# Attention's sink products: two passes over 128 rows in place of three over 64

## The chip, the cores and the metric

The kernel runs on one core of a Trainium2 chip. The metric is the device time of one execution in microseconds (us), as the median of several runs. The engines are named as in the profile: PE is TensorE (matmuls), PEld its weight loads, DVE is VectorE, ACT is ScalarE, POOL is GpSimd, SP issues most DMAs. Each engine runs its own instructions in the order in which the program gives them, and waits on semaphores for the others.

## The reference

Three stages follow each other: attention with a window and sinks, a mixture of experts weighted by a Sinkhorn iteration, and a top-1 mixture of experts. Only the first is touched:

```python
# q, k, v: (2, 8, 768, 64); n_sink = 4, window = 128
scores = scale * np.matmul(q, k.transpose(0, 1, 3, 2))
keep = is_sink | in_window          # pos < n_sink, or 0 <= row - col < window
scores = np.where(keep, scores, -1e9)
a = np.exp(scores - np.max(scores, axis=-1, keepdims=True))
a = a / (np.sum(a, axis=-1, keepdims=True) + 1e-09)
attn_out = np.matmul(a, v)
```

The two mixtures then work on `attn_out` as 1536 tokens of 512 numbers, with 8 experts of 512x1024 and 1024x512 each.

## The kernel before

**High and low parts.** A product of two fp32 operands is made of three matmuls in fp32r. Each operand is kept as a high part (a copy rounded to fp32r, made by ACT or DVE) and a low part (operand minus high part, made by DVE or POOL). `mm3` (lines 65 to 68) then adds low x high (line 66), high x low (67) and high x high (68) into one PSUM tile. Every product in attention and in the mixtures goes through it, so lines 66 to 68 stand for all matmuls of this kind, and one tells them apart by the tiles.

**Attention** runs over 12 blocks of 128 queries (6 in each of the 2 batches), and in each block over 4 pairs of heads. One pair is one step `m`, 48 in all. From the third block of a batch on, a query sees 128 + 128 window keys and SK = 16 sink keys, so the scores are 272 wide (256 or 128 wide before). A step is spread over several turns of the loop (lines 1201 to 1245): in the turn of `m`, PE does

1. `pv(m - 5)`, the products of the probabilities with the values, into the one PSUM tile `pv`. It takes four heads of a group, two in each of two turns (part 0 and part 1). After part 1, ACT copies it to `xh` (line 1172) and DVE makes `xl` from it; the next part 0 can't start ahead of that, since it writes the same tile;
2. `p_trans(m - 3)`, four transposes of P into `tr`, after which ACT makes the high part and DVE the low part (tiles called `pt` or `acc` in the profile);
3. in odd turns `s_trans(m - 2)` (line 1138), the transpose of the sink columns `pk` of four heads at once into the PSUM tile L1; in even turns the transposes of the next block's k or q (line 1003), through the same PSUM tile L1. ACT makes `skh`, `kh` or `qh` from it, DVE makes `skl`, `kl` or `ql`; only after that is L1 free for the next transpose;
4. `scores(m)`, six matmuls for two heads (`sc`), from which DVE takes the row minimum (line 1096) and ACT the exponential (line 1100).

The subtractions for the low parts are not emitted where they arise but gathered (`defer`) and emitted by `flush()` (line 992) after `pv` and `norm`, and again after `scores`. `norm(m - 1)` has DVE make the reciprocal of the row sums (lines 1108, 1109), POOL multiply P by it (line 1111) and POOL copy the 16 sink columns of the two heads into `pk` (line 73, called by `pcopy`).

**The sink products.** For each head of a block with sinks, `pv` adds the 16 sink keys' share as one more `mm3` (line 1164): the stationary operand is `vsh` or `vsl`, 64 rows (4 heads x 16 sinks, of which only the own head's 16 rows hold values, the others zero) by 64 columns; the moving operand is `skh` or `skl`, 64 rows by 128 queries. There are 2 batches x 4 blocks x 8 heads = 64 heads of this kind. `vsh` and `vsl` are made once a batch by `prep_vs`.

**Fills.** In turns from `m` = 21 on, the first mixture's matmuls (tiles `L` and `y`, 512 columns) stand between attention's, one group of three in five of six places of two turns (line 1295). Ahead of that, and in a turn where a unit has ended, PE has attention alone. What is left of these units, and all that follows, comes after attention.

Of the kernel before, what the change touches and what calls it, by code (L numbers as in the profile page):

```python
# [8 lines left out]
F32 = mybir.dt.float32  # L9
F32R = mybir.dt.float32r  # L10
I32 = mybir.dt.int32
AF = mybir.ActivationFunctionType
ALU = mybir.AluOpType
# [10 lines left out]
def kernel(  # L24
# [15 lines left out]
    nc = tc.nc  # L40
    B, H, S, D = q.shape
# [9 lines left out]
    SK = 16  # L51
# [11 lines left out]
    ps_m = ctx.enter_context(tc.tile_pool(name="ps_m", bufs=1, space=PSUM))  # L63

    def mm3(out_ap, ah, al, bh, bl, start, stop):
        nc.tensor.matmul(out_ap, al, bh, start=start, stop=False)  # L66
        nc.tensor.matmul(out_ap, ah, bl, start=False, stop=False)  # L67
        nc.tensor.matmul(out_ap, ah, bh, start=False, stop=stop)  # L68

    def pcopy(dst, src):  # L70
        a = src if src.dtype == F32 else src.bitcast(F32)
        o = one[0:a.shape[0], :].unsqueeze(2).to_broadcast(list(a.shape))
        nc.gpsimd.tensor_tensor(dst, a, o, op=ALU.mult)

    def ctile(shape, name, dt=F32):
        return const.tile(shape, dt, name=name)
# [3 lines left out]

    ident = ctile([128, 128], "ident")
    one = ctile([128, 1], "one")
    rflag = ctile([128, 1], "rflag")
    iof = ctile([128, 128], "iof")
    x2d = dram.tile([N, DM], F32, name="x2d")
# [718 lines left out]
    a1 = att.enter_context(tc.tile_pool(name="a1", bufs=1))  # L804
    a2 = att.enter_context(tc.tile_pool(name="a2", bufs=2))
# [183 lines left out]
    def defer(*args):  # L989
        later.append(args)  # L990
# [6 lines left out]
    kt, qt, vt, vs = [], {}, {}, {}  # L997
# [52 lines left out]
        return r  # L1050

    def prep_vs(b, r):
        sh = a1.tile([4 * SK, 2, 4, D], F32R, name="vsh")
        sl = a1.tile([4 * SK, 2, 4, D], F32R, name="vsl")
        full = accp.tile([4 * SK, 2, 4, D], F32, name="acc7")
        for g in range(2):
            nc.gpsimd.tensor_tensor(
                full[:, g], r[:, g, :].unsqueeze(1).to_broadcast([4 * SK, 4, D]),
                bdiag.unsqueeze(2).to_broadcast([4 * SK, 4, D]), op=ALU.mult,
            )  # L1060
        vs[b] = sh, sl

        def fin():
            nc.vector.tensor_copy(sh, full)
            nc.vector.tensor_tensor(sl, full, sh.bitcast(F32), op=ALU.subtract)
            acc[7] = accp.tile([128, DM], F32, name="acc7")

        return fin

    P, sums, pts = {}, {}, {}  # L1070

    def width(i):
        return (128, 256, 256 + SK)[min(i, 2)]

    def where(m):
        blk, pr = divmod(m, 4)
        b, i = divmod(blk, NB)
        return blk, b, i, pr
# [25 lines left out]
    def norm(m):  # L1104
        blk, b, i, pr = where(m)
        w = width(i)
        rs = a3.tile([128, 2], F32, name="rs")
        nc.vector.tensor_scalar(rs, sums.pop(m), 1e-9, None, op0=ALU.add)
        nc.vector.reciprocal(rs, rs)
        p = P[m][:, :, 0:w]  # L1110
        nc.gpsimd.tensor_tensor(p, p, rs.unsqueeze(2).to_broadcast([128, 2, w]), op=ALU.mult)
        if i >= 2:
            if pr % 2 == 0:
                pts[m // 2, "k"] = a2.tile([128, 4, SK], F32, name="pk")
            o = 2 * (pr % 2)
            pcopy(pts[m // 2, "k"][:, o:o + 2, :], P[m][:, :, 128:128 + SK])

    def p_trans(m):
        blk, b, i, pr = where(m)
# [12 lines left out]
    def s_trans(m):  # L1132
        blk, b, i, pr = where(m)
        if i < 2:
            return
        pk = pts.pop((m // 2, "k"))
        ph = ps_m.tile([4 * SK, 128], F32, name="L1", tag="L1")
        nc.tensor.transpose(ph, pk.rearrange("p h s -> p (h s)"), ident)
        th = a2.tile([4 * SK, 128], F32R, name="skh")
        tl = a2.tile([4 * SK, 128], F32R, name="skl")  # L1140
        nc.scalar.activation(th, ph, AF.Copy)
        defer(tl, ph, th)
        pts[m // 2, "s"] = th, tl

    def pv(m):
        blk, b, i, pr = where(m)
        g, part = divmod(pr, 2)
        o = pvt
        sink = i >= 2
        nch = 1 if i == 0 else 2  # L1150
        th, tl = pts.pop(m)
        for hh in range(2):
            j = 2 * part + hh
            hs = slice((4 * g + j) * D, (4 * g + j + 1) * D)
            for c in range(nch):
                vh, vl = vt[blk if c == nch - 1 else blk - 1]
                mm3(
                    o[:, j, :], vh[:, hs], vl[:, hs], th[:, hh, c, :], tl[:, hh, c, :],
                    c == 0, c == nch - 1 and not sink,
                )  # L1160
            if sink:
                sth, stl = pts[m // 2, "s"]
                sh, sl = vs[b]
                mm3(o[:, j, :], sh[:, g, j, :], sl[:, g, j, :], sth, stl, False, True)
        if part == 0:
            return
        c, t = divmod(blk, TPC)
        cs = slice(t * 128, (t + 1) * 128)
        for r in range(2):
            ps = slice(64 * r, 64 * r + 64)  # L1170
            oh = xh[c][ps, 2 * g:2 * g + 2, cs]
            nc.scalar.activation(oh, o[:, r::2, :], AF.Copy)
            defer(xl[c][ps, 2 * g:2 * g + 2, cs], o[:, r::2, :], oh)
# [4 lines left out]
    def attention():  # L1178
# [22 lines left out]
        for m in range(NM + LV):  # L1201
            blk, pr = divmod(m, 4)
            if m >= LV:
                pv(m - LV)
            if 1 <= m <= NM:
                norm(m - 1)
# [4 lines left out]
            if 2 < m <= NM + 1 and m % 2 == 1:  # L1211
                s_trans(m - 2)
# [19 lines left out]
            if m % (4 * NB) == 8:  # L1232
                vfin = prep_vs(blk // NB, vsr.pop(blk // NB))
# [216 lines left out]
```

## Time and profile before

| | us |
|---|---|
| median of 3 runs | 1479.87 (1479.65 to 1479.95) |
| profiled execution, its own time | 1480.35 |
| its span, first to last instruction | 1478.6 |
| PE busy | 1442.5 (98% of the span) |
| DVE busy | 695.2 (47%) |
| ACT busy | 455.5 (31%) |
| POOL busy | 129.8 (9%) |

Attention takes the first 206 us of the span; in it the sink products stand from 51.9 us (batch 0, to 109.7 us) and from 141.6 us (batch 1, to 204.4 us). The fills begin at 79.0 us. The busy time of PE counts each matmul from its start to the end of its way through the array. Matmuls overlap, so the cost of one in a row of them is the distance from its start to the next one's start, and that is read from the timeline, not from the duration.

In the profile a matmul's form such as `128*64 128x128` means: 128 rows and 64 columns of the array in use, and 128 partitions by 128 columns streamed through it.

### The profile page before, as it was taken

The page shows a single profiled execution, that of the slowest core. Times are in us where ns is not written, and L with a number is a line of the kernel's source. Part 1 is how long each engine was busy: PE and PEld are TensorE (multiplying, and loading weights), DVE is VectorE, ACT ScalarE, POOL GpSimd, SP SyncE. Part 2 cuts the span into 40 slices and gives each one's busy share as a digit, 9 for nine tenths or more (in the row PEclk, how much of TensorE's full clock was granted, in tenths as well). Part 3 has the DMA queues.
Part 4 walks back from the last instruction along what each step waited for, and adds up shares of the span by engine and source line. Part 5 has one row for each costly group of instructions (what it writes and reads, how often), then busy time and mean ns, then how long its engine had stood idle before and what let it go on. Part 6 is the DMA issues. An engine that isn't in the chain of part 4 may idle for free. (4 is left out here: it accounts for less than half of the span.)

```text
span 1478.6 us, 18476 instructions
## 1 busy us (share of the span) xinstructions
PE 1442.5 (98%) x7245; PEld 1178.2 (80%) x7245; DVE 695.2 (47%) x1487; ACT 455.5 (31%) x966; POOL 129.8 (9%) x188
## 2 busy tenths in 40 slices
PE   5899999999999999999999999999999999899998
PEld 4777787788888888888888888888888877788886
DVE  5868643553323333332423333242333257877774
ACT  4756532111202211120211112021111133666664
POOL 3634310000000000000000000000000000111111
PEclk9999999999999999999999999999999999999999
DMA  5412102000101010010101000010100041987771
GB/s 110 95 44 59 44 30 86 29 29 29 57 0 58 0 57 29 29 51 7 58 1 57 28 30 31 27 57 1 57 0 0 29 143 44 327 278 263 269 259 56
DMA packets 86029, 105.69 MB, mean 71 GB/s; under 512 B 41518, under 2 KB 41518, under 8 KB 85936
## 3 DMA queue, kind: packets, MB, share of 16 engines
q1 hardware_dynamic: 83056, 96.58, 20.4%
q0 software_dynamic: 2880, 7.87, 1.6%
q8 instruction: 59, 0.97, 0.3%
q14 instruction: 34, 0.28, 0.1%
HBM read 101.29 MB, written 7.86 MB: 74 GB/s over the span
## 5 line engine op out<-in xcount | busy, mean ns | idle before, releaser
L192 ACT ACTIVATE hh<-L 128x512 fp32r<-128x512 f32 x192 | 114.8, 598 | 802.0 <-PE L L68 801.9
L193 DVE SCALAR_TENSOR_TENSOR hl<-L,hh 128x512 fp32r<-128x512 f32 x192 | 132.8, 692 | 355.9 <-ACT hh L192 355.7
L216 DVE SCALAR_TENSOR_TENSOR acc<-y,Pm,acc 128x512 f32<-128x512 f32 x168 | 126.1, 751 | 252.3 <-PE y L68 251.9
L66 PE MATMUL y<-whb,hl 128*128 128x512 f32 x432 | 170.8, 395 | 0.0
L68 PE MATMUL y<-whb,hh 128*128 128x512 f32 x432 | 168.6, 390 | 0.0
L67 PE MATMUL y<-wlb,hh 128*128 128x512 f32 x432 | 168.2, 389 | 0.0
L66 PE MATMUL y<-wha,hl 128*128 128x512 f32 x412 | 163.0, 396 | 0.1
L68 PE MATMUL y<-wha,hh 128*128 128x512 f32 x412 | 160.6, 390 | 0.0
L67 PE MATMUL y<-wla,hh 128*128 128x512 f32 x412 | 160.5, 390 | 0.0
L66 PE MATMUL L<-xh,wla 128*128 128x512 f32 x384 | 152.8, 398 | 0.0
L66 PE MATMUL L<-xh,wlb 128*128 128x512 f32 x384 | 151.0, 393 | 0.0
L68 PE MATMUL L<-xh,wha 128*128 128x512 f32 x384 | 149.7, 390 | 0.0
L68 PE MATMUL L<-xh,whb 128*128 128x512 f32 x384 | 149.6, 390 | 0.0
L67 PE MATMUL L<-xl,wha 128*128 128x512 f32 x384 | 149.6, 390 | 0.0
L67 PE MATMUL L<-xl,whb 128*128 128x512 f32 x384 | 149.6, 390 | 0.0
L68 PEld LDWEIGHTS y<-whb,hh 128*128 128x128 f32 x432 | 81.1, 188 | 17.2
L67 PEld LDWEIGHTS y<-wlb,hh 128*128 128x128 f32 x432 | 81.2, 188 | 16.0
L66 PEld LDWEIGHTS y<-whb,hl 128*128 128x128 f32 x432 | 81.2, 188 | 16.0
L688 POOL DMA_INDIRECT acc<-x2d,ig_s x2 | 2.1, 1051 | 1045.7 <-DVE tmp_d L439 1020.5
L68 PEld LDWEIGHTS y<-wha,hh 128*128 128x128 f32 x412 | 77.4, 188 | 16.1
L66 PEld LDWEIGHTS y<-wha,hl 128*128 128x128 f32 x412 | 77.4, 188 | 15.8 <-DVE acc L210 0.2
L67 PEld LDWEIGHTS y<-wla,hh 128*128 128x128 f32 x412 | 77.5, 188 | 15.0
(313 smaller groups left out, 2358.2 us busy)
## 6 DMA issues: line engine op xcount, KB each, us to landing
raw<-in_moe_w SPq DMA_DIRECT2D x80, 1024.0 KB, 5.5
raw<-in_v SPq DMA_DIRECT2D x12, 256.0 KB, 2.9
raw<-vfb SPq DMA_DIRECT2D x12, 256.0 KB
x2d<-acc SPq DMA_DIRECT2D x12, 256.0 KB, 2.0
raw<-in_k SPq DMA_DIRECT2D x11, 256.0 KB
raw<-in_q SPq DMA_DIRECT2D x11, 256.0 KB, 6.1
raw<-in_k SPq DMA_DIRECT2D x2, 128.0 KB
raw<-in_q SPq DMA_DIRECT2D x2, 128.0 KB
```

What stands on the lines that cost most here:

```text
L66: nc.tensor.matmul(out_ap, al, bh, start=start, stop=False)
L67: nc.tensor.matmul(out_ap, ah, bl, start=False, stop=False)
L68: nc.tensor.matmul(out_ap, ah, bh, start=False, stop=stop)
L192: nc.scalar.activation(hh, ps, AF.Relu)
L193: nc.vector.scalar_tensor_tensor(hl, ps, 0.0, hh.bitcast(F32), op0=ALU.max, op1=ALU.subtract)
L216: nc.vector.scalar_tensor_tensor(a, ps, Pm[:, blk, e:e + 1], a, op0=ALU.mult, op1=ALU.add)
L688: nc.gpsimd.indirect_dma_start(out=x, out_offset=None, in_=src, in_offset=bass.IndirectOffsetOnAxis(ap=index(ig_s, ig_d, i), axis=0))
```

## The change

The values of the sinks are kept in one tile `vsk` of 128 rows: rows 0 to 63 hold the high parts, rows 64 to 127 the low parts. POOL writes the sink probabilities twice into `pk` (now 2 x 4 x 16 = 128 columns), so that the transpose gives 128 rows, in which rows 64 to 127 repeat rows 0 to 63; `skh` and `skl` have 128 rows each. A product of all 128 rows with `skl`, and one with `skh`, added up, gives (high + low) x low + (high + low) x high. So each head has two matmuls of 128 rows by 64 columns, first with `skl`, then with `skh`, where there were three of 64 by 64. The product low x low, left out before, is in it.

```diff
     def prep_vs(b, r):
-        sh = a1.tile([4 * SK, 2, 4, D], F32R, name="vsh")
-        sl = a1.tile([4 * SK, 2, 4, D], F32R, name="vsl")
+
+        t = a1.tile([128, 2, 4, D], F32R, name="vsk")
...
-            nc.vector.tensor_copy(sh, full)
-            nc.vector.tensor_tensor(sl, full, sh.bitcast(F32), op=ALU.subtract)
+            hi = t[0:4 * SK]
+            nc.vector.tensor_copy(hi, full)
+            nc.vector.tensor_tensor(t[4 * SK:128], full, hi.bitcast(F32), op=ALU.subtract)
...
-                pts[m // 2, "k"] = a2.tile([128, 4, SK], F32, name="pk")
+                pts[m // 2, "k"] = a2.tile([128, 2, 4, SK], F32, name="pk")
             o = 2 * (pr % 2)
-            pcopy(pts[m // 2, "k"][:, o:o + 2, :], P[m][:, :, 128:128 + SK])
+            pk = pts[m // 2, "k"][:, :, o:o + 2, :]
+            src = P[m][:, :, 128:128 + SK].unsqueeze(1).to_broadcast([128, 2, 2, SK])
+            nc.gpsimd.tensor_tensor(pk, src, one3.to_broadcast([128, 2, 2, SK]), op=ALU.mult)
...
-        ph = ps_m.tile([4 * SK, 128], F32, name="L1", tag="L1")
-        nc.tensor.transpose(ph, pk.rearrange("p h s -> p (h s)"), ident)
-        th = a2.tile([4 * SK, 128], F32R, name="skh")
-        tl = a2.tile([4 * SK, 128], F32R, name="skl")
+        ph = ps_m.tile([128, 128], F32, name="L1", tag="L1")
+        nc.tensor.transpose(ph, pk.rearrange("p c h s -> p (c h s)"), ident)
+        th = a2.tile([128, 128], F32R, name="skh")
+        tl = a2.tile([128, 128], F32R, name="skl")
...
-                sth, stl = pts[m // 2, "s"]
-                sh, sl = vs[b]
-                mm3(o[:, j, :], sh[:, g, j, :], sl[:, g, j, :], sth, stl, False, True)
+                for n, a in enumerate(pts[m // 2, "s"][::-1]):
+                    nc.tensor.matmul(o[:, j, :], vs[b][:, g, j, :], a, start=False, stop=n == 1)
```

No instruction changes its place but for the sink matmuls themselves. On PE, in the third head with sinks and the start of the fourth, in the order of the program (engine PE, `pv` of one turn; `pt_1211` and `acc_1212` are the high and low part of the transposed probabilities), before:

```order
L66 MATMUL pv<-pt_1211,vl 64x128
L67 MATMUL pv<-acc_1212,vh 64x128
L68 MATMUL pv<-pt_1211,vh 64x128
L66 MATMUL pv<-skh,vsl 64x128
L67 MATMUL pv<-skl,vsh 64x128
L68 MATMUL pv<-skh,vsh 64x128
L66 MATMUL pv<-pt_1211,vl 64x128
L67 MATMUL pv<-acc_1212,vh 64x128
```

And now, at the same place (`pt_1208` and `acc_1209` are the same two tiles):

```order
L66 MATMUL pv<-pt_1208,vl 64x128
L67 MATMUL pv<-acc_1209,vh 64x128
L68 MATMUL pv<-pt_1208,vh 64x128
L1167 MATMUL pv<-skl,vsk 64x128
L1167 MATMUL pv<-skh,vsk 64x128
L66 MATMUL pv<-pt_1208,vl 64x128
L67 MATMUL pv<-acc_1209,vh 64x128
```

One of three sink matmuls is gone, and the first of the two left reads `skl`, which DVE writes, where the first of the three read `skh`, which ACT writes.

## Rows read from the trace of the kernel before

**Rows 1.** The page's first part: busy us, share of the span, instructions of each engine.

```profile
PE 1442.5 (98%) x7245; PEld 1178.2 (80%) x7245; DVE 695.2 (47%) x1487; ACT 455.5 (31%) x966; POOL 129.8 (9%) x188
```

**Rows 2.** PE's timeline, first sink head: start, duration, tiles, rows*columns, idle before.

```profile
51.78 0.23 PE L68 MATMUL pv<-acc,vh 128*64 128x128 f32 x1
51.94 0.27 PE L66 MATMUL pv<-skh,vsl 64*64 64x128 f32 x1
52.05 0.22 PE L67 MATMUL pv<-skl,vsh 64*64 64x128 f32 x1
...
52.25 0.28 PE L66 MATMUL pv<-acc,vl 128*64 128x128 f32 x1
52.37 0.22 PE L67 MATMUL pv<-acc,vh 128*64 128x128 f32 x1
52.43 0.22 PE L68 MATMUL pv<-acc,vh 128*64 128x128 f32 x1
```

**Rows 3.** Stretches: busy us and (instructions) of tile skh alone, clock, DMA.

```profile
51.40:77.40 26.00, 6.23 (x32) 3.97 (x32) 1.09 (x4) 1.03 (x4) 1.00 0.29 64
```

**Rows 4.** PE's timeline in two turns without fills.

```profile
57.91 0.24 PE L66 MATMUL pv<-pt,vl 128*64 128x128 f32 x1 [0.22 <-DVE xl L994]
...
58.39 0.27 PE L66 MATMUL pv<-skh,vsl 64*64 64x128 f32 x1
...
60.02 0.27 PE L1138 MATMUL L<-ident,pk 128*64 128x128 f32 x1
```

**Rows 5.** DVE's timeline in the same turns.

```profile
55.89 0.27 DVE L994 TENSOR_TENSOR skl<-L,skh 64x128 fp32r<-64x128 f32 x1
...
56.92 0.85 DVE L994 TENSOR_TENSOR xl<-pv,xh 64x256 fp32r<-64x256 f32 x2 [0.28 <-ACT xh L1172]
...
59.16 0.68 DVE L994 TENSOR_TENSOR ql<-L,qh 128x512 fp32r<-128x512 f32 x1
```

**Rows 6.** ACT's timeline in the same turns.

```profile
55.98 0.18 ACT L1100 ACTIVATION_READ_ACCUMULATOR P<-P,nm 128x1 f32 x1
56.12 0.76 ACT L1172 ACTIVATE xh<-pv 64x256 fp32r<-64x256 f32 x2
```

**Rows 7.** PE's timeline, transposes of pk where fills stand between, and around them.

```profile
80.23 0.27 PE L1138 MATMUL L<-ident,pk 128*64 128x128 f32 x1
...
89.33 0.27 PE L1138 MATMUL L<-ident,pk 128*64 128x128 f32 x1
...
97.86 0.60 PE L1126 MATMUL tr<-ident,P 128*128 128x128 f32 x4
98.30 0.27 PE L1138 MATMUL L<-ident,pk 128*64 128x128 f32 x1
...
143.59 0.27 PE L1138 MATMUL L<-ident,pk 128*64 128x128 f32 x1
```

**Rows 8.** DVE's timeline, the subtractions that free L1 for those four transposes.

```profile
78.91 0.68 DVE L994 TENSOR_TENSOR kl<-L,kh 128x512 fp32r<-128x512 f32 x1
...
88.50 0.68 DVE L994 TENSOR_TENSOR ql<-L,qh 128x512 fp32r<-128x512 f32 x1
...
97.30 0.68 DVE L994 TENSOR_TENSOR kl<-L,kh 128x512 fp32r<-128x512 f32 x1
...
142.76 0.68 DVE L994 TENSOR_TENSOR kl<-L,kh 128x512 fp32r<-128x512 f32 x1
```

**Rows 9.** POOL's timeline, one copy into pk.

```profile
57.98 0.24 POOL L73 TENSOR_TENSOR pk<-P,one 128x32 f32<-128x32 f32 x1
```

**Rows 10.** Groups of DVE by line and form, 0 to 215 us: busy us, mean ns.

```profile
L994 DVE TENSOR_TENSOR xl<-pv,xh 64x256 fp32r<-64x256 f32 x48 | 20.0, 417 | 7.1 <-ACT xh L1172 5.8
...
L994 DVE TENSOR_TENSOR acc<-tr,pt 128x256 fp32r<-128x256 f32 x6 | 2.5, 420 | 0.0
```

**Rows 11.** Stretches, all instructions: length, PE, PEld, DVE, ACT, POOL busy (x), clock.

```profile
20.00:51.40 31.40, 23.52 (x183) 18.87 (x183) 26.21 (x99) 22.11 (x68) 21.86 (x32) 0.89 0.55 131
51.40:77.40 26.00, 24.98 (x245) 20.01 (x246) 21.00 (x75) 20.66 (x60) 16.98 (x23) 1.00 0.29 64
```

More of the change, by code (lines that the diff above doesn't have):

```diff
@@ L82 @@
     one = ctile([128, 1], "one")
+    one3 = one.unsqueeze(2).unsqueeze(3)
     rflag = ctile([128, 1], "rflag")
@@ L1060, in prep_vs @@
             )
-        vs[b] = sh, sl
+        vs[b] = t
         def fin():
-            nc.vector.tensor_copy(sh, full)
-            nc.vector.tensor_tensor(sl, full, sh.bitcast(F32), op=ALU.subtract)
+            hi = t[0:4 * SK]
+            nc.vector.tensor_copy(hi, full)
+            nc.vector.tensor_tensor(t[4 * SK:128], full, hi.bitcast(F32), op=ALU.subtract)
             acc[7] = accp.tile([128, DM], F32, name="acc7")
```

## The prediction, made blind

> **What bounds the kernel now.** I read the page's first part first: PE is busy for 98% of the span, no other engine for more than 47% [rows 1]. So time taken from PE counts, unless PE then waits. A busy share doesn't tell whether it would: attention is one stage of 206 us out of 1478.6, and in it PE hangs on DVE and ACT turn by turn. So next I read PE's timeline around a sink head for what the three passes cost from start to start [rows 2]; the number of sink heads in the stretch in which PE has attention alone [rows 3]; and, in that stretch and in the others, how long before PE's start the last thing it needs was done [rows 4 to 8]. Where that distance is about 0.14 us, PE started as soon as it could: that is what is left after xl's end at 56.92 + 0.85 = 57.77, when pv starts at 57.91 with a wait shown [rows 4, 5]. Where the distance is larger, what exceeds 0.14 is free.
>
> **One head.** From the last window product at 51.78 to the second product after the sinks at 52.37 it takes 0.59 us, in five steps: 0.16 into the sinks, 0.11 between the first two passes, then 0.20 for the third and the way out, then 0.12 [rows 2]. A step between two products of one form is 0.06 (52.37 to 52.43). Nothing is waited for there; what differs is the form, 128*64 outside and 64*64 inside. So each change of the number of rows costs about 0.15 on its two steps together, twice a head, and a pass itself 0.06. After the change all are 128*64: four steps of 0.06, 0.24. **A head costs 0.59 - 0.24 = 0.35 us less**, six times the pass that goes. That is 64 x 0.35 = 22.4 us of PE's time, if every follower of a sink head behaves like this one.
>
> **What PE can't keep, without fills.** 32 matmuls of skh in 51.4 to 77.4 us, two a head, are 16 heads in eight turns [rows 3]. There two chains through other engines stand close behind PE.
> - Before a part 0 of pv: at 56.12 ACT starts the copies from pv, as its exponential's last read ends at 55.98 + 0.18 = 56.16; xl follows to 57.77, and pv at 57.91 has waited 0.22 for it [rows 4 to 6]. An earlier end of the two heads before it would only find ACT still at the exponential, which hangs on the scores of the turn before.
> - In the next turn: ql ends at 59.16 + 0.68 = 59.84 and frees L1, pk's transpose starts at 60.02 [rows 4, 5]. 0.18 less 0.14 leaves 0.04 free. DVE comes to ql by way of the row minima and the low part of P, which hang on the scores of the turn before.
>
> So each turn gives back nearly all of its 2 x 0.35: in one the wait for xl grows from 0.22 to about 0.9, in the other a wait of 0.66 arises at pk. What is left is what both chains gain by starting a little earlier, at most 0.1 in a pair of turns by the distances above: 0.4 in all, of 16 x 0.35 = 5.6. Bounds: 0 and 5.6; I take 0.4, since both distances are read directly.
>
> **What PE can keep, with fills.** The other 48 heads give 48 x 0.35 = 16.8. Fills stand between pv and the waiting points, so most distances there are long. Four transposes of pk are the exceptions, each with two heads (0.70) before it. Distance from the end of kl or ql: 80.23 - 79.59 = 0.64, so 0.50 free, 0.20 lost; 89.33 - 89.18 = 0.15, nothing free, 0.70 lost; 98.30 - 97.98 = 0.32, 0.18 free, 0.52 lost; 143.59 - 143.44 = 0.15, 0.70 lost [rows 7, 8]. Together 2.1. Six later transposes of pk have sinks and fills ahead of them; I count them as free (the other case is a rival).
>
> **What is added.**
> - POOL's copy into pk, 0.24 now [rows 9], writes twice the elements, 32 times. It can double at most by that, 7.7 us of POOL's time; nothing of it counts: queued behind it on POOL is the next multiplication of P, and PE reads pk at 60.02, 1.8 us after the end at 58.22 [rows 4, 9]. POOL is busy for 17.0 of 26.0 us there [rows 11]. Without that cover it would cost 0.24 a pk.
> - ACT and DVE take skh and skl from 128 partitions instead of 64, the same 128 elements each: 417 ns for 256 elements on 64 partitions and 420 ns on 128 [rows 10], so nothing, between 0 and a doubling of 16 x 0.27 on DVE [rows 5], 4.3 us, a part of it on the chain.
> - The first sink pass now reads skl. DVE ends it at 55.89 + 0.27 = 56.16, the first pass stands at 58.39 [rows 4, 5]: 2.2 us early, so no wait.
> - pk's transpose has 128 columns instead of 64. Four transposes of 128*128 up to pk, 97.86 to 98.30, are 0.44 or 0.11 each, and inside the run it is (0.60 - 0.27) / 3 = 0.11 as well [rows 7]: the number of columns changes nothing.
>
> **The sum** against the profiled execution (1480.35, span 1478.6): 16.8 - 2.1 + 0.4 = 15.1, so 1465.2. The median of the runs shown is 0.5 lower, 1479.87; the same 15.1 off it gives **1464.8**. What follows attention is PE's own, and moves forward as it is.
>
> **Rivals.**
> - *No wait takes it back.* All 64 heads count: 22.4 less, 1457.5. For it: PE is 98% busy, and other work on DVE could be done in the time. Against it: the distances of 0.14 to 0.18 in rows 4, 5, 7 and 8.
> - *The fills don't cover either.* All ten transposes of pk behind sinks and among fills lose their 0.70, since a low part of a fill (DVE) falls ahead of kl or ql as it does at 88.50: 7.0 lost instead of 2.1, so 10.2 in all, 1469.7. For it: two of the four that I name are at the bound already. Against it: the later ones stand behind one or two groups of fills.
> - *The change of rows isn't the cause.* The long steps around the sinks stay, for instance because they come from reading other tiles, and only the pass goes: 48 x 0.06 = 2.9, about 1477.0. Against it: the long step stands on both sides, also where the next product reads the same tiles as the one before, and nothing is waited for.
> - *A change of columns costs as much as one of rows.* Then the 16 transposes of pk, now of the form of those before them, save another 16 x 0.15 = 2.4: 1462.4. Against it: 0.11 before pk as inside the run [rows 7]. The Trainium skill, TensorEngine Tiling (Array Packing), section Key Properties, says that a change of the tiling mode, and not just of the tile, drains TensorE, and lists 128x128 and 128x64 as two modes; by that rule it would be this rival's time. The trace agrees for rows 64 and 128, and not for columns.
> - *Slower: the clock.* PE waits more in 51 to 77 us. In 20 to 51 us, where it was busy for 23.5 of 31.4 us (75%), the granted clock was 0.89 on the mean, so lower for a part of it; in 51.4 to 77.4, at 25.0 of 26.0, it was 1.00 [rows 11]. Afterwards I expect (25.0 - 5.6) / 25.6 = 76%, near the first. The first's mean alone would cost 0.11 x 26 = 2.9: 1467.7. It ends slower than before if the clock falls to half (1.2 GHz) from 51 us on and stays there: 19.4 us of work become 38.8, 13.2 above the stretch's 25.6, and some 4 us more of PE's work at half clock among the fills use up the 15.1. Held to 110 us it is 27 more, 1505. Against it: matmuls still come in every turn, and the longest wait becomes 0.9 us.
>
> **How the numbers follow.** Forecast 1464.8 (losses as counted, and a few short stretches of lower clock within it, to about 1468): 0.66. No wait at all, 1457.5: 0.08. Fills don't cover, 1469.7: 0.12. Columns, 1462.4: 0.04. Only the pass, 1477.0: 0.06. Slower by the clock: 0.04. The range reaches from 1460.5 (the part of the 5.6 and 2.1 that may come back after all, short of 1457.5) to 1471.5 (fills don't cover, and a little of the clock or of skl's eviction); it leaves out the first rival, the third and the last, 0.18. A difference under 0.2%, 3.0 us, is about what a measurement of this kernel can't tell from none: the third rival lies on that edge and is halved between faster and same. Faster 0.66 + 0.08 + 0.12 + 0.04 + 0.03 = 0.93, same 0.03, slower 0.04.
>
> **What would show it.** In the profile after: 128 matmuls of 128*64 with vsk, each step around them 0.06, a head within 0.24; if the steps stay at 0.11 to 0.16, the cause is wrong. Without fills, waits for xl of about 0.9 before pv and new waits for kl and ql before pk, the eight turns still some 25.6 us long; if they take 21, the chains were not the bound. With fills, the last sink product at about 190 us instead of 204; 194 would mean that the fills don't cover. PEclk below 1.00 between 51 and 110 us would show the last rival. A new wait on POOL or for skl on PE would show that an added cost isn't covered.

## The result and the profile after

| | before | after |
|---|---|---|
| median of 4 runs, us | 1479.77 (1479.65 to 1479.95) | 1465.45 (1465.06 to 1466.54) |
| profiled execution, its own time | 1480.35 | 1465.45 |
| its span | 1478.6 | 1463.7 |
| PE busy | 1442.5 | 1422.5 |

The ratio is 0.9902 with a 95% interval of 0.9889 to 0.9914: 14.3 us faster by the medians, where 15.1 less, at 1464.8, was forecast.

The first part of the page after, with the columns of [rows 1]: 64 matmuls fewer and 20 us less of PE's busy time; POOL has 1.9 us more, DVE the same as before.

```profile
PE 1422.5 (97%) x7181; PEld 1164.8 (80%) x7181; DVE 695.2 (47%) x1487; ACT 454.6 (31%) x966; POOL 131.7 (9%) x188
```

PE's timeline, the first sink head of after (answers to [rows 2]). The last window product at 50.76 and the second product after the sinks at 51.00 lie 0.24 us apart, in four steps of 0.06; before it was 0.59 in five.

```profile
50.44 0.24 PE L66 MATMUL pv<-acc,vl 128*64 128x128 f32 x1 [0.43 <-DVE xl L995]
...
50.76 0.23 PE L68 MATMUL pv<-acc,vh 128*64 128x128 f32 x1
50.82 0.22 PE L1167 MATMUL pv<-skl,vsk 128*64 128x128 f32 x1
50.88 0.22 PE L1167 MATMUL pv<-skh,vsk 128*64 128x128 f32 x1
50.94 0.22 PE L66 MATMUL pv<-acc,vl 128*64 128x128 f32 x1
51.00 0.22 PE L67 MATMUL pv<-acc,vh 128*64 128x128 f32 x1
```

The tile of the sink values and, for before, that of the high parts of the probabilities: duration of a matmul in ns (min/median/max), start of the first and of the last in us. From the first sink matmul to the last of this kind it took 152.3 us before and takes 138.1 now.

```profile
L1167 PE MATMUL pv<-skl,vsk x64: 218/222/226, 50.8 to 188.9; 128*64 128x128 f32 x64
```

```profile
L66 PE MATMUL pv<-skh,vsl x64: 269/271/273, 51.9 to 204.2; 64*64 64x128 f32 x64
```

Groups of PE in the turns without fills (after 51 to 76 us; before 51.4 to 77.4 us): after the bar busy time and mean ns, then the idle time before the group and what ended it. The only waits of before are those for xl, in two groups of 0.7 and 0.4 us. After the change xl stands at 0.8 and 0.4, and three others have come: 1.7 before the transposes of pk, 1.0 before those of `raw` (the next keys and queries), 0.5 for ACT.

```profile
L66 PE MATMUL pv<-pt,vl 128*64 128x128 f32 x21 | 4.8, 249 | 0.7 <-DVE xl L994 0.7
...
L66 PE MATMUL pv<-acc,vl 128*64 128x128 f32 x12 | 2.7, 244 | 0.4 <-DVE xl L994 0.4
```

```profile
L66 PE MATMUL pv<-pt,vl 128*64 128x128 f32 x21 | 4.6, 236 | 1.3 <-DVE xl L995 0.8 <-ACT kh L1006 0.5
...
L1004 PE MATMUL L<-ident,raw 128*128 128x128 f32 x16 | 2.6, 287 | 1.0 <-DVE skl L995 1.0
...
L66 PE MATMUL pv<-acc,vl 128*64 128x128 f32 x10 | 2.1, 230 | 0.4 <-DVE xl L995 0.4
...
L1142 PE MATMUL L<-ident,pk 128*128 128x128 f32 x4 | 1.2, 300 | 1.7 <-DVE rs L1110 1.7
```

Two of those waits in DVE's and PE's timeline of after. `ql` ends at 58.00 + 0.68 = 58.68 and pk's transpose starts 0.15 later; the profile names `rs`, which overlaps ql's end on DVE, but it is ql that frees L1: at 130.59, where the profile names ql, the distance from its end is the same 0.15. `skl` ends at 61.45, and the transposes of `raw`, which write the same L1, start at 61.51, only 0.06 later. So the 0.14 that the prediction took for the shortest distance holds before pv and pk, and not for every instruction of PE.

```profile
58.00 0.68 DVE L995 TENSOR_TENSOR ql<-L,qh 128x512 fp32r<-128x512 f32 x1
...
61.17 0.28 DVE L995 TENSOR_TENSOR skl<-L,skh 128x128 fp32r<-128x128 f32 x1
```

```profile
58.83 0.30 PE L1142 MATMUL L<-ident,pk 128*128 128x128 f32 x1 [0.44 <-DVE rs L1110]
...
61.51 0.66 PE L1004 MATMUL L<-ident,raw 128*128 128x128 f32 x4 [0.24 <-DVE skl L995]
```

The four transposes of pk behind fills that the prediction named (answers to [rows 7]), the first with no idle time shown:

```profile
78.36 0.30 PE L1142 MATMUL L<-ident,pk 128*128 128x128 f32 x1
...
86.81 0.30 PE L1142 MATMUL L<-ident,pk 128*128 128x128 f32 x1 [0.54 <-DVE rs L1110]
...
94.94 0.30 PE L1142 MATMUL L<-ident,pk 128*128 128x128 f32 x1 [0.32 <-DVE rs L1110]
...
138.31 0.30 PE L1142 MATMUL L<-ident,pk 128*128 128x128 f32 x1 [0.80 <-DVE rs L1110]
```

Stretches of after (columns as in [rows 11]). In the stretch without fills PE is busy for 20.26 of 24.60 us (82%), at a clock of 1.00 there and up to the end of attention; among the fills PE is 95 to 99% busy.

```profile
20.00:51.40 31.40, 22.48 (x199) 17.93 (x200) 26.66 (x100) 22.62 (x70) 22.98 (x32) 0.95 0.54 121
51.40:76.00 24.60, 20.26 (x217) 15.99 (x214) 19.91 (x71) 19.70 (x58) 16.38 (x22) 1.00 0.31 67
76.00:105.00 29.00, 28.09 (x255) 22.56 (x256) 20.46 (x73) 17.87 (x56) 11.42 (x16) 1.00 0.25 56
105.00:136.00 31.00, 29.52 (x233) 22.52 (x232) 27.24 (x86) 19.86 (x58) 16.44 (x25) 1.00 0.24 52
136.00:192.00 56.00, 55.20 (x494) 45.73 (x494) 38.42 (x125) 31.81 (x92) 23.77 (x42) 1.00 0.17 45
```

### The profile page after: what moved, and what is told of

It reads as the page before. It is cut to its first block, busy times and chain, and to the rows that moved or that the text cites. A ratio compares the mean times of both kernels' runs of the same rounds, so it can differ in the third digit from the quotient of the medians.

```text
span 1463.7 us, 18342 instructions
## 1 busy us (share of the span) xinstructions
PE 1422.5 (97%) x7181; PEld 1164.8 (80%) x7181; DVE 695.2 (47%) x1487; ACT 454.6 (31%) x966; POOL 131.7 (9%) x188
## 5 line engine op out<-in xcount | busy, mean ns | idle before, releaser
L68 PEld LDWEIGHTS y<-wha,hh 128*128 128x128 f32 x412 | 77.3, 188 | 16.2
L66 PEld LDWEIGHTS y<-wha,hl 128*128 128x128 f32 x412 | 77.4, 188 | 15.3 <-DVE acc L211 0.2
```

## The experiments

A time hangs also on what comes before and behind the sinks (below), so beside each median stands the time from the first sink matmul to the last, read from PE's timeline, in which the disputed steps lie. The runs of before that stand beside the experiments have medians of 1480.1 to 1480.3.

| kernel | median, us | ratio to before, 95% | first sink to last, us |
|---|---|---|---|
| before | 1479.77 | | 152.4 |
| after | 1465.45 | 0.9902 [0.9889, 0.9914] | 138.2 |
| e1_three_128 | 1467.63 | 0.9912 [0.9896, 0.9929] | 140.4 |
| e2_two_64 | 1477.97 | 0.9977 [0.9967, 0.9987] | 149.4 |
| e7_additions_alone | 1480.17 | 0.9999 [0.9989, 1.0009] | 152.7 |
| e3_pk_own_bank | 1462.66 | 0.9881 [0.9864, 0.9897] | 135.7 |
| e3_again | 1462.53 | 0.9880 [0.9863, 0.9896] | 135.7 |
| e9_before_own_bank | 1480.09 | 1.0010 [0.9999, 1.0020] | 152.5 |
| e4_two_pv | 1465.86 | 0.9901 [0.9885, 0.9918] | 138.2 |
| e5_both | 1463.11 | 0.9880 [0.9863, 0.9896] | 136.0 |
| e10_own_bank_by_phase | 1463.64 | 0.9887 [0.9871, 0.9904] | 134.8 |

**Is it the pass or the change of rows?** The changed kernel had two differences at once: a pass fewer, and 128 rows throughout. One kernel takes back the pass alone, the other takes it away alone.

```diff
-                for n, a in enumerate(pts[m // 2, "s"][::-1]):
-                    nc.tensor.matmul(o[:, j, :], vs[b][:, g, j, :], a, start=False, stop=n == 1)
+                for n, a in enumerate((zt, *pts[m // 2, "s"][::-1])):
+                    nc.tensor.matmul(o[:, j, :], vs[b][:, g, j, :], a, start=False, stop=n == 2)
```

> The changed kernel with a third pass of 128 rows in front of the two, whose moving operand is a tile of zeros. Theory (a change of rows costs about 0.15 on each side, a pass 0.06): a head takes 0.30 us from the last window product to the second after the sinks, against 0.24 changed and 0.59 before; 48 heads keep it, so 2.9 us above the changed kernel's 1465.5: 1468.4. Rival (the gain comes from the number of passes): three passes again, so most of the 14.3 us is lost, 1477 to 1480.

Measured 1467.63 (1467.48 to 1468.25), 2.2 us above after: 0.8 less than the theory gave, and 9 off the rival. Its timeline: the third pass adds a step of 0.06, and all steps stay at 0.06.

```profile
54.17 0.23 PE L68 MATMUL pv<-pt,vh 128*64 128x128 f32 x1
54.23 0.23 PE L1169 MATMUL pv<-zt,vsk 128*64 128x128 f32 x1
54.29 0.22 PE L1169 MATMUL pv<-skl,vsk 128*64 128x128 f32 x1
54.35 0.22 PE L1169 MATMUL pv<-skh,vsk 128*64 128x128 f32 x1
54.41 0.22 PE L66 MATMUL pv<-pt,vl 128*64 128x128 f32 x1
```

Before, with a pass fewer and 64 rows as they were:

```diff
-                mm3(o[:, j, :], sh[:, g, j, :], sl[:, g, j, :], sth, stl, False, True)
+                nc.tensor.matmul(o[:, j, :], sh[:, g, j, :], stl, start=False, stop=False)
+                nc.tensor.matmul(o[:, j, :], sh[:, g, j, :], sth, start=False, stop=True)
```

> The kernel before without the pass of low values by high probabilities: two passes over 64 rows. The low part of the sink values is left out. Theory: the changes of rows stay, a head takes 0.53 instead of 0.59, 48 x 0.06 = 2.9 us less than before: 1476.9. Rival (number of passes): about the changed kernel's 1465.5.

Measured 1477.97 (1475.98 to 1479.05), some 2 us below before, 1.1 above the theory's figure and 12 above the rival; from the first sink to the last 3.0 us less. The long steps stay on both sides of the pair: 0.16 and 0.11 going in, 0.15 and 0.10 coming out.

```profile
52.53 0.22 PE L68 MATMUL pv<-acc,vh 128*64 128x128 f32 x1
52.69 0.27 PE L1164 MATMUL pv<-skl,vsh 64*64 64x128 f32 x1
52.80 0.22 PE L1165 MATMUL pv<-skh,vsh 64*64 64x128 f32 x1
52.95 0.27 PE L66 MATMUL pv<-acc,vl 128*64 128x128 f32 x1
53.05 0.23 PE L67 MATMUL pv<-acc,vh 128*64 128x128 f32 x1
```

What follows: of the 14.3 us a pass is worth 2 to 3 (2.2 by the one, 3.0 by the other), the uniform number of rows 11 to 12. Three passes of 128 rows (140.4 us from sink to sink) are 9 us quicker than two of 64 (149.4). "The change of rows isn't the cause" falls.

**Do the additions cost or bring anything?** Before, with pk written twice, its transpose, `skh` and `skl` with 128 partitions, and the three passes of 64 rows kept (they read the first 64 rows):

```diff
-                pts[m // 2, "k"] = a2.tile([128, 4, SK], F32, name="pk")
+                pts[m // 2, "k"] = a2.tile([128, 2, 4, SK], F32, name="pk")
...
-        ph = ps_m.tile([4 * SK, 128], F32, name="L1", tag="L1")
+        ph = ps_m.tile([128, 128], F32, name="L1", tag="L1")
...
-                sth, stl = pts[m // 2, "s"]
+                sth, stl = (x[0:4 * SK] for x in pts[m // 2, "s"])
```

> The kernel before with all that the change adds and without what it removes: pk written twice, transpose and skh and skl over 128 partitions, but three passes over the first 64 rows with vsh and vsl as before. Theory (the additions are covered): 1479.8, within 0.5. Rival (the copies or evictions cost, and the passes bring more than seen): 1481 to 1484.

Measured 1480.17 (1479.44 to 1481.75) beside 1480.32 of before. POOL's copy of twice the elements takes 0.29 instead of 0.24 [rows 9], `skl` on 128 partitions 0.28 instead of 0.27 [rows 5]. The additions cost nothing that can be measured, and 128 columns in pk's transpose bring nothing. A change of columns alone can be seen in the changed kernel too: from the last sink product (128*64) to the transposes of P (128*128) the step is 0.07, as within a run, and the step behind it 0.13, where the next ones are 0.11.

```profile
57.65 0.22 PE L1167 MATMUL pv<-skl,vsk 128*64 128x128 f32 x1
57.70 0.23 PE L1167 MATMUL pv<-skh,vsk 128*64 128x128 f32 x1
57.77 0.62 PE L1130 MATMUL tr<-ident,P 128*128 128x128 f32 x4
```

The Trainium skill, TensorEngine Tiling (Array Packing), section Key Properties, has TensorE drained by any change of the tiling mode; 128x128 and 128x64 are among the modes that the page lists. The runs agree for rows (0.15 us a change on its two steps) and not for columns (0.03 at most on the two steps). Whether the forms in the profile are the page's modes, no run here shows.

**Where does the gain of the first 16 heads go?** The theory is that L1 and xl, both behind DVE, hold PE. So pk's transpose goes to a bank that the fills don't use at that moment, which takes away what made it wait:

```diff
     def l1(g, c, f):
...
+        cnt["free"] = "y0"
...
     def l2(g, c, t):
...
+        cnt["free"] = "L0"
...
-        ph = ps_m.tile([128, 128], F32, name="L1", tag="L1")
+        ph = ps_m.tile([128, 128], F32, name="L1", tag=cnt["free"])
```

> The changed kernel, with the transpose of pk in the PSUM tile that the fills don't use at the time (y0 or L0) instead of L1. Theory (L1, shared with the transposes of k and q, takes the time back): the waits for kl and ql before pk (0.6 to 0.7 in each second turn without fills, and 0.2 to 1.0 at four places with fills) and those for skl before the transposes of k and q (0.4) go. With fills 2.4 us come back. Without fills the wait for xl stays and grows, but a pair of turns falls from 6.35 to about 5.85, over four pairs 2 more: about 1461. Rival (DVE itself is full there): the stretch without fills stays as long, 1463 to 1465.5.

Measured 1462.66 (1462.52 to 1464.03), and 1462.53 (1462.37 to 1462.86) as e3_again: 2.8 us below after, near the rival's lower end and not at 1461. But the rival's reason doesn't hold, since the stretch without fills did get shorter. Of the 2 us forecast there 1.5 came, of the 2.4 with fills 1.0. In the turns without fills the waits before pk and `raw` are gone, and those for xl have grown from 1.2 to 4.2 us in the sum (groups of PE in e3_again, 51 to 76 us). The 16 heads take 21.1 us from the first to the sixteenth instead of 22.6.

```profile
L66 PE MATMUL pv<-pt,vl 128*64 128x128 f32 x24 | 5.1, 235 | 3.3 <-DVE xl L997 3.3
...
L66 PE MATMUL pv<-acc,vl 128*64 128x128 f32 x9 | 1.9, 231 | 0.9 <-DVE xl L997 0.9
```

A part of what kept it from 1461: where the kind of fill changes, the next fill takes the bank that pk had just been given, and waits for `skl` (PE of e3_pk_own_bank; 0.97 and 0.70 idle).

```profile
136.59 0.50 PE L66 MATMUL L<-xh,wla 128*128 128x512 f32 x1 [0.97 <-DVE skl L997]
...
168.04 0.50 PE L66 MATMUL y<-wha,hl 128*128 128x512 f32 x1 [0.70 <-DVE skl L997]
```

> e3_pk_own_bank once more, beside e10_own_bank_by_phase on one chip: 1462.7 us, so that the two differ by the choice of the bank alone.

The same bank in the kernel before, chosen as in e5_both and e10_own_bank_by_phase, where the bank changes at the end of a kind of fill:

```diff
+        if f == FB - 1:
+            cnt["free"] = "L0"
...
+            if t == TPC - 1:
+                cnt["free"] = "y0"
...
-        ph = ps_m.tile([4 * SK, 128], F32, name="L1", tag="L1")
+        ph = ps_m.tile([4 * SK, 128], F32, name="L1", tag=cnt["free"])
```

> The kernel before (three passes over 64 rows) with pk's transpose in the tile that the fills have just left. Theory (before the change L1 was at its bound but hid behind PE's own work, and only the change brought the wait out): only the waits that stood there before go, 0.8 at the second batch's first transposes and 0.3 after, about 1.2: 1478.6. Rival (L1 held the kernel before as much as after): 3 to 4 us less, 1476.

Measured 1480.09 (1479.36 to 1484.20 in 10 runs, four of them above 1483.6, with a mean clock of 0.992 to 0.996 where the others have 0.997 to 1.000), and from sink to sink 152.5, as before: neither figure. In the turns without fills nothing is gained (25.91 us from the first head to the 17th, 25.89 before): there pk's transpose was just free [rows 4, 5], and its wait is one that the change brought. Two waits of before at later transposes of pk, at 135.90 and 143.59, are gone, but one with a fill's bank took their place, 1.34 us behind the transposes ahead of it:

```profile
178.90 0.27 PE L1142 MATMUL L<-ident,pk 128*64 128x128 f32 x1 [1.07 <-DVE hl L193]
```

**Is xl the next one?** In after, with L1 as it is, every second group of pv gets a bank of its own in the turns without fills, so that it doesn't wait for xl's reading of the bank before:

```diff
+    pvo = [pvt]
...
-        o = pvt
+        if part == 0 and pr % 2 == 0:
+            two = m + LV <= 19 and m // 2 % 2
+            pvo[0] = ps_m.tile([D, 4, 128], F32, name="L", tag="L0") if two else pvt
+        o = pvo[0]
```

> The changed kernel, with every second group of pv in the PSUM tile L0 in the turns ahead of the fills (turns 5 to 19), so that part 0 need not wait for xl. pk's transpose stays in L1. Theory (two chains hold PE there, xl and L1, one after the other): the waits for xl go, 0.45 to 0.6 in each of four pairs of turns with sinks, and up to 3 us in the turns before the first sinks, where they are 0.5 to 2.3; the waits for kl and ql before pk stay or grow. 1460 to 1464. Rival (DVE or ACT are full there): 1465.5.

Measured 1465.86 (1465.14 to 1466.79): no gain, and from the first sink head to the 17th 25.53 us, as in after (25.55). Where pv no longer waits for xl, pk waits for `ql` by so much longer: 0.86 idle, where after shows 0.44 at 58.83.

```profile
59.27 0.30 PE L1142 MATMUL L<-ident,pk 128*128 128x128 f32 x1 [0.86 <-DVE rs L1110]
```

> The changed kernel with both: pv in two PSUM tiles ahead of the fills, and pk's transpose in the tile that the fills have just left (chosen at the end of a fill's tiles, so that a new phase of fills doesn't wait for skl, as it did for 1.2 and 0.9 us in the run with pk's own tile). Theory: without fills a pair of turns falls from 5.72 us, with pk's own tile alone, to DVE's own work of about 5.2; with fills 2 us more come back: 1457 to 1459.5. Rival (pk's own tile alone had taken what there is): 1462.7 less the 2 us at the phases, 1460.5.

Both edits together, the bank chosen as in e9_before_own_bank. Measured 1463.11 (1461.84 to 1464.16), no better than e3_pk_own_bank; a miss. Where L1 and the bank of pv no longer hold it, pv waits for `vl`, which POOL makes behind another conversion (`wla`), as long as it waits for xl at that place in e3_pk_own_bank (the last of the three rows):

```profile
60.87 1.45 POOL L168 TENSOR_TENSOR wla<-raw,wha 128x512 fp32r<-128x512 f32 x1
62.29 1.26 POOL L1048 TENSOR_TENSOR vl<-raw,vh 128x512 fp32r<-128x512 f32 x1
```

```profile
63.60 0.27 PE L66 MATMUL pv<-pt,vl 128*64 128x128 f32 x1 [1.70 <-POOL vl L1048]
```

```profile
62.70 0.25 PE L66 MATMUL pv<-pt,vl 128*64 128x128 f32 x1 [1.63 <-DVE xl L997]
```

Besides, the profiled execution of this kernel (1464.16, the slowest of its four) has a clock of 0.86 in the stretch without fills, where after and e3_again have 1.00:

```profile
51.00:76.00 25.00, 22.72 (x228) 19.26 (x227) 21.39 (x74) 20.03 (x59) 17.29 (x22) 0.86 0.30 66
```

How much of the missed gain is one and how much the other isn't settled.

> The changed kernel, pk's transpose in a bank that the fills don't use at that moment: the bank is chosen at the end of a fill's last tile (L0 behind the last tile of the first kind of fill, y0 behind the last of the second), not at its start. It differs from e3_pk_own_bank by that choice alone and from e5_both by leaving every pv group in its one bank. Theory (e5_both was not better than e3_pk_own_bank because a second pv bank there only moved the wait: its pv groups waited up to 1.9 us for POOL): the two waits where the kind of fill changes in e3_pk_own_bank, 1.19 us at 136.59 and 0.93 us at 168.04, go, and nothing else moves: 1462.7 - 2.1 = 1460.5 us. Rival (the two waits only stood in place of waits that come right behind them): 1462.5 to 1463.

This is e5_both without the second bank of pv. Measured 1463.64 (1461.91 to 1464.04), above both figures, beside 1462.53 of e3_again on the same chip. Of the 2.1 us from sink to sink 0.9 came (134.8 against 135.7). The two waits for `skl` are gone, but a transpose of pk now waits for a fill's low part `hl` (DVE), which frees the bank given to it, as in e9_before_own_bank:

```profile
164.81 0.69 DVE L194 SCALAR_TENSOR_TENSOR hl<-L,hh 128x512 fp32r<-128x512 f32 x1 [1.04 <-ACT hh L193]
```

```profile
165.65 0.30 PE L1146 MATMUL L<-ident,pk 128*128 128x128 f32 x1 [1.07 <-DVE hl L194]
```

The 0.9 isn't seen in the median; the profiled execution is the quickest of this kernel's four, and what the other three lost, 1.7 us, stays open. Against after, e3_pk_own_bank is the quickest version by its two medians: all its eight runs (1462.37 to 1464.03) lie below the four of after (1465.06 to 1466.54). They did not stand beside after on one chip, and the intervals of the ratios to before overlap.

## Why the prediction was right

**One head.** 0.59 - 0.24 = 0.35 was forecast. Over all 64 heads of either trace the distance over the sinks shrank from 42.9 to 21.3 us, 21.6 against 22.4, or 0.34 a head. Its split, 0.06 for the pass and the rest for the rows, is borne out by e1_three_128 and e2_two_64.

**Without fills.** 0.4 of 5.6 was forecast to stay. From the first head to the 17th it was 25.89 us (51.94 to 77.83) and is 25.55 (50.82 to 76.37): 0.34. The waits came where they were named, before pv and before pk, but not in the sizes named. The prediction had about 0.66 added in each pair of turns at either place, 2.6 in all at each. Measured from start to start, 2.3 came at pk, but only 0.7 at pv: xl's wait is 0.38 or 0.39 there and not about 0.9, and one of these waits is for ACT (kh). Another 1.6 came at a wait that wasn't named: `raw` for `skl`, four times. It isn't a price of `skl`'s 128 partitions (e7_additions_alone), but PE arriving earlier at the same L1. As the prediction put it, "a new wait [...] for skl on PE would show that an added cost isn't covered": that reading was too narrow. The total was right all the same, since both chains together set the length of a pair of turns, wherever the wait shows: freeing xl's bank alone brings nothing (e4_two_pv), and freeing L1 alone gives back 1.5 of the 5.0 lost here (the 16 heads alone shrank by 5.4) and leaves xl to hold the rest, with waits of 0.84 to 1.64 (e3_again). The split between the two was wrong.

**With fills.** 16.8 - 2.1 = 14.7 was forecast. From the 17th head to the last sink matmul it was 126.54 us (77.83 to 204.37) and is 112.61 (76.37 to 188.98): 13.9. The way into the 17th head and the last head's way out, 0.1 each, lie outside that: 14.1. The steps before the four transposes of pk grew to 0.33, 0.82, 0.59 and 1.08, where one without a wait is 0.11: 0.22, 0.71, 0.48 and 0.97. Before, the fourth's step was 0.42 already, so it lost 0.65. That is 2.06 together against the 2.1 of the sum. "The fills don't cover" (10.2 in all) falls: the last sink product starts at 188.98, where about 190 was forecast and 194 would have been that rival's sign. The 0.6 that is missing is the 0.01 by which a head was taken too high, 48 times: these heads shrank by 16.2 and not by 16.8. That is the one term of the sum that was mis-sized.

**Additions.** Nothing was forecast, and e7_additions_alone measured nothing: 1480.17 beside 1480.32.

**The sum.** 15.1 was forecast; the two traces give 0.34 + 13.9 + 0.2 = 14.5 between the last window product ahead of the first sinks and the way out of the last. The spans differ by 14.9. That window product stands 1.0 us earlier (50.76 and 51.78), of which 0.75 is there already at the first product of the scores (12.73 and 13.48), ahead of anything that the change touches. And about 0.6 is lost again behind attention. Of that, 0.4 is one longer wait for ACT, at the same place of the program (before, then after):

```profile
1267.35 0.66 PE L727 MATMUL h2p<-ident,hl 128*128 128x128 f32 x4 [0.26 <-ACT hl L716]
```

```profile
1252.34 0.66 PE L728 MATMUL h2p<-ident,hl 128*128 128x128 f32 x4 [0.68 <-ACT hl L717]
```

In after ACT is still at two conversions of weights there, for which it has waited 1.96 us (`raw` from a DMA). A stretch at half clock, which after has at 1235 us and before hasn't at this place, isn't the cause: matmul for matmul, after leads by 15.4 us ahead of it and by 15.4 again at 1246.

So the agreement of 14.9 with 15.1 is in part luck; 14.5 in attention and 14.3 between the medians are the fairer comparison.

**The rivals.** No wait at all (1457.5): waits came. Columns (1462.4): e7_additions_alone and the step of 0.07 speak against it. The clock: 1.00 from 51.4 to 192 us, although PE is busy for less of the time (82%, forecast 76%).

## What to carry to other kernels

A short product with fewer rows of the array than its neighbours can cost more by the change of rows, on the way in and out, than by itself; filling the rows, here with the low parts, was worth about four to five and a half times the pass that it saved. To see what is kept of such a gain, read at each later wait of the engine how long its operand had been done: where the distance is already the shortest that the trace shows for such an instruction (here 0.15 us before a transpose of pk, 0.06 before one of `raw`), the gain becomes a wait there, or at the next place that hangs on the same chain. And freeing one of two such chains is worth testing alone, in both orders: here one brought 2.8 us, and the other nothing.

## What was not expected of the hardware

The granted clock falls to half (1.2 GHz) for stretches of a few us, up to 17 us in one trace, at places that differ from trace to trace with the same work there. In the kernel e10_own_bank_by_phase the mean in 20 to 51 us is 0.67, in e3_again, which differs from it only by which bank pk is given, 0.89, and in e9_before_own_bank 1.00 (the first and the last of these):

```profile
20.00:51.00 31.00, 25.67 (x190) 20.75 (x191) 25.64 (x99) 22.19 (x68) 22.49 (x32) 0.67 0.53 122
```

```profile
20.00:51.00 31.00, 21.21 (x188) 17.21 (x189) 26.91 (x101) 21.95 (x68) 22.53 (x32) 1.00 0.56 130
```

Whether the kernel sets these places or the single execution isn't settled: e3_pk_own_bank and e3_again, one kernel, have them within 0.2 us of each other.

The mean says little about the time, as PE waits for other engines there anyway. From the first product of the scores to the first sink matmul it takes 38.07 us in e10_own_bank_by_phase, 37.85 in e3_again and 37.75 in e9_before_own_bank. It takes longest, 39.13 and 39.66, in e7_additions_alone and e2_two_64, where the clock is at half until just before the first sinks (to 52.1 and 52.5 us). The row of e2_two_64:

```profile
46.00:52.40 6.40, 5.94 (x37) 4.92 (x38) 4.82 (x17) 3.71 (x10) 3.77 (x5) 0.50 0.76 202
```

The first product of the scores itself stands at 12.60 to 13.48 us. Together this moves the first sink matmul by up to 2 us from one trace to the next (50.63 to 52.69 over all kernels here), as much as some of the differences that were to be measured. That is why the time from sink to sink stands beside the medians.
